# Row maxima that read scores from PSUM, a last maximum over four transposes, and another split of the eight PSUM banks

## The chip, the cores and the metric

The kernel runs on one core of a Trainium2 chip. The core has a matrix engine (TensorE, PE in the rows; its weight loads are PEld), a vector engine (VectorE, DVE), a scalar engine (ScalarE, ACT), a general engine (GpSimd, POOL) and an engine that issues DMAs (SyncE, SP). Matrix products land in PSUM, which this kernel uses as eight banks of 128 partitions by 512 fp32 columns. The metric is device time in microseconds, lower is better.

## The reference, cut to what matters

Three layers follow each other: an attention in which a query sees only keys of the same hash bucket, a gated layer, and a layer with a leaky rectifier.

```python
q_bits = einsum('bhsd,dk->bhsk', q, proj) > 0        # 6 bits; the same for k
mask   = q_bucket[..., :, None] == k_bucket[..., None, :]
scores = where(mask, scale * q @ k.T, -1e9)          # batch 2, 8 heads, 768 x 768, d = 64
attn   = exp(scores - scores.max(-1)) ; attn /= attn.sum(-1) + 1e-9
x      = (attn @ v)          -> 1536 tokens x 512
g      = x @ w_gate          # 512 x 1536
x      = (g * sigmoid(g) * (x @ w_val)) @ w_out      # 1536 x 512
h      = x @ w_in            # 512 x 2048
out    = (max(h, 0) + alpha * min(h, 0)) @ w_out2    # 2048 x 512
```

What the change touches is `scores.max(-1)`: the largest score of each query over its 768 keys.

## The kernel before

**Units.** An attention unit is one head and 256 queries: 48 units, two of them (`x` = 0 and 1) making an item of a head pair. `s_bank` computes scores transposed, keys on partitions and queries along columns: three PSUM banks `S` (j = 0, 1, 2) of 128 x 2 x 256, each of four matmuls (L282, L283), and after each bank ScalarE copies it into the SBUF tile `se` (L284). `s_max` then takes on VectorE the larger of the columns of banks 0 and 1 (L288), with a floor the larger of that and bank 2 (L289), both over 512 columns and both reading `se`, and folds the two halves of 256 columns into one (L291). `s_mt` transposes that result on TensorE, two 128 x 128 transposes (L297, tile `mt`), and a reduction over 256 columns (L299) gives the maximum of each query (`mq`). `s_mb` transposes `mq` back as a broadcast (L304, tile `mb`), `s_sub` subtracts it from `se` (L309, 1536 columns), `s_exp` takes the exponential (L314), and `s_pv` multiplies by the values into `po` (L321, two instructions for each fp32 matmul). The tile `m2`, which holds the maxima, has one buffer; `se` has four.

**Stages.** Tokens go in three chunks of 512. First, attention alone works on chunk 0 (units 0 to 15). Then the gated layer of chunk 0 runs with the attention of chunk 1 between its matmuls, and the gated layer of chunk 1 with the attention of chunk 2 (`RATES` says how many attention steps go with each step of the layer). After that come the gated layer of chunk 2, with no attention left, and the last layer of all three chunks. Below, the stretches are called first (14 to 136 us of the profile), second (136 to 340), third (340 to 495), fourth (495 to 617) and fifth (617 to the end).

**PSUM banks.** A tile takes a bank by its tag, and the next tile of a tag waits until a bank of that tag is free. Before: tag S has two banks, M one, G two, Y two, po one. Scores take S, S, M. In the first stretch `mt` and `mb` take G, the hash products `hp` take po, and `po` takes Y. From the second stretch on, `mt`, `mb` and `hp` all take S, so two banks serve two thirds of the scores and all of these; gates take G (2) and values Y (2), and the products of the gated layer's second weight alternate between them.

**What sets the order.** The kernel is written in Python with the tile framework. The program's text gives each instruction a priority; the framework's scheduler then places the instructions of each engine in a fixed queue, waiting for free buffers and banks, and adds the semaphores. Each engine works through its queue strictly in order. So a change of banks also moves instructions in the queues.

## Time and profile before

| | us |
|---|---|
| median of 3 runs | 887.34 (886.62 to 889.05) |
| the profiled execution, its own time | 884.68 |
| its span, first to last instruction | 882.8 |
| TensorE busy, whole span | 827.7 (94%) |
| VectorE busy | 559.6 (63%) |
| ScalarE busy | 449.3 (51%) |
| GpSimd busy | 373.8 (42%) |

The profiled execution lies 2.66 us below the median of the runs, and 1.9 us of its own time lie outside its span. Busy shares are means over stretches with different limits: TensorE is busy all of the third and fifth stretch, while in the first two VectorE and ScalarE are busy for most of the time as well. A busy TensorE is not TensorE at its peak, since matmuls overlap and their ends are modelled; the distance from the start of one to the start of the next tells what one costs.

### The profile page before, as it was taken

How to read it: one execution, taken by the hardware profiler on the slowest of the kernel's cores; microseconds unless marked ns; L12 is line 12 of the kernel's file. 1: busy time of each engine (PE TensorE's matmuls, PEld its weight loads, DVE VectorE, ACT ScalarE, POOL GpSimd, SP SyncE). 2: the span in 40 equal slices, each digit the busy share in tenths (PEclk: the TensorE clock that was granted, in tenths of full speed). 3: DMA queues.
4: the chain of work that ended last, by engine and by line, in shares of the span. 5: the costliest groups of instructions: out<-in, count | busy, mean ns of one | idle time of the engine just before them, and what ended most of it. 6: DMA issues, size and time to landing. Idle time of an engine off the chain costs nothing.

```text
span 882.8 us, 11030 instructions
## 1 busy us (share of the span) xinstructions
PE 827.7 (94%) x3952; PEld 685.9 (78%) x3952; DVE 559.6 (63%) x824; ACT 449.3 (51%) x738; POOL 373.8 (42%) x304
## 2 busy tenths in 40 slices
PE   5988769988989999999999998999999999999998
PEld 3777658867777788888888787877888888888886
DVE  5788989997789976776767355554633353334332
ACT  6787767577666565555554232413433333334331
POOL 4221443766555443342221354534544454445441
PEclk9999989999999999999999999999999999999999
DMA  9111343775755535745444668878000300010001
GB/s 221 42 45 60 127 160 128 217 236 214 235 199 192 179 131 191 240 148 195 168 179 152 218 253 295 294 282 281 2 1 1 130 14 1 1 48 1 1 1 48
DMA packets 57286, 122.01 MB, mean 138 GB/s; under 512 B 16912, under 2 KB 29200, under 8 KB 56720
## 3 DMA queue, kind: packets, MB, share of 16 engines
q1 hardware_dynamic: 56080, 118.51, 39.3%
q0 software_dynamic: 1008, 2.75, 1.5%
q8 instruction: 31, 0.51, 0.2%
q14 instruction: 23, 0.19, 0.1%
q10 hardware_dynamic: 144, 0.05, 0.0%
HBM read 94.03 MB, written 27.26 MB: 137 GB/s over the span
## 4 chain that ended last, share of the span: by engine, by line
PE 69%; DVE 12%; ACT 7%; DMA 7%; issue 3%; POOL 1%; SPq 0%; DVEq 0%; ACTq 0%; POOLq 0%
PE po L321 9%; PE gp L628 7%; PE gp L629 7%; PE gp L627 7%; PE op L632 5%; PE hp L627 5%; PE hp L628 5%; PE op L633 5%; PE op L634 5%; PE hp L629 5%; PE S L283 2%; DMA raw<-in_wblk_dram 2%; PE S L282 2%; DMA wb<-w 2%; ACT se L314 2%
## 5 line engine op out<-in xcount | busy, mean ns | idle before, releaser
L622 POOL TENSOR_TENSOR gl<-ex,gh 128x512 fp32r<-128x512 f32 x84 | 111.7, 1330 | 182.8 <-ACT gh L619 182.6
L321 PE MATMUL po<-se,vv 128*128 128x256 f32 x576 | 145.9, 389 | 8.6 <-ACT se L314 8.6
L321 PEld LDWEIGHTS po<-se,vv 128*128 128x128 f32 x576 | 107.5, 194 | 26.2 <-ACT se L314 11.4
L627 PE MATMUL gp<-xh,wb 128*128 128x512 f32 x288 | 122.4, 426 | 2.9 <-DMA wb<-w 2.9
L613 DVE TENSOR_SCALAR ex<-hp,al 128x512 f32<-128x512 f32 x48 | 36.0, 751 | 134.8 <-PE hp L629 134.7
L629 PE MATMUL gp<-xh,wb 128*128 128x512 f32 x288 | 114.7, 398 | 0.0
L628 PE MATMUL gp<-xl,wb 128*128 128x512 f32 x288 | 113.9, 396 | 0.1
L619 ACT ACTIVATE gh<-ex 128x512 fp32r<-128x512 f32 x84 | 53.0, 631 | 114.9 <-DVE ex L616 68.4
L529 POOL TENSOR_TENSOR wt<-wt,wr 128x512 int32<-128x512 int32 x48 | 65.5, 1368 | 100.3 <-DVE wt L527 56.5
L564 ACT ACTIVATE wb<-w 128x512 fp32r<-128x512 f32 x96 | 60.4, 631 | 91.8 <-PE hp L629 77.8
L314 ACT ACTIVATE se<-se 128x1536 f32<-128x1536 f32 x48 | 71.3, 1485 | 48.9 <-DVE se L309 48.7
L284 ACT ACTIVATE se<-S 128x512 f32<-128x512 f32 x144 | 80.4, 592 | 25.8 <-PE S L283 22.4
L282 PE MATMUL S<-QA,kt 128*128 128x256 f32 x288 | 82.0, 313 | 9.9 <-ACT se L284 6.2
L309 DVE SCALAR_TENSOR_TENSOR se<-se,mb 128x1536 f32<-128x1536 f32 x48 | 83.7, 1744 | 2.3 <-PE mb L304 2.2
L283 PE MATMUL S<-qb,kt 76*128 76x256 f32 x288 | 75.8, 292 | 3.4 <-ACT qb L204 2.6
L627 PE MATMUL hp<-xh,wb 128*128 128x512 f32 x192 | 74.7, 389 | 0.0
L628 PE MATMUL hp<-xl,wb 128*128 128x512 f32 x192 | 74.7, 389 | 0.0
L629 PE MATMUL hp<-xh,wb 128*128 128x512 f32 x192 | 74.7, 389 | 0.0
L632 PE MATMUL op<-wb,gh 128*128 128x512 f32 x192 | 74.7, 389 | 0.0
L633 PE MATMUL op<-wb,gh 128*128 128x512 f32 x192 | 74.7, 389 | 0.0
L634 PE MATMUL op<-wb,gl 128*128 128x512 f32 x192 | 74.7, 389 | 0.0
L571 POOL TENSOR_TENSOR wb<-w,wb 128x512 fp32r<-128x512 f32 x48 | 61.9, 1289 | 24.1 <-ACT wb L564 24.1
(95 smaller groups left out, 1707.0 us busy)
## 6 DMA issues: line engine op xcount, KB each, us to landing
wb<-w SPq DMA_DIRECT2D x72, 512.0 KB, 4.3
raw<-in_wblk_dram SPq DMA_DIRECT2D x68, 512.0 KB, 4.0
w<-wb SPq DMA_DIRECT2D x36, 512.0 KB, 2.9
qr<-in_q_dram SPq DMA_DIRECT2D x24, 256.0 KB, 2.9
nat<-in_k_dram SPq DMA_DIRECT2D x8, 384.0 KB, 4.5
vv<-in_v_dram SPq DMA_DIRECT2D x16, 192.0 KB, 4.9
whole<-wt SPq DMA_DIRECT2D x12, 256.0 KB, 2.2
w<-whole SPq DMA_DIRECT2D x12, 256.0 KB, 5.7
```

The lines of the kernel that those rows point to most:

```text
L282: nc.tensor.matmul(pt[:, i, :], lhsT=ka[:, sl], rhs=qa, start=True, stop=False)
L283: nc.tensor.matmul(pt[:, i, :], lhsT=kb[:, sl], rhs=qb, start=False, stop=True)
L309: nc.vector.scalar_tensor_tensor(out=u.se, in0=u.se, scalar=FLOOR, in1=u.mx[:, None, :].to_broadcast([P, NC, GQ]), op0=ALU.max, op1=ALU.su ...
L314: nc.scalar.activation(out=u.se, in_=u.se, func=AF.Exp, scale=SCALE)
L321: nc.tensor.matmul(it.po[:, u.x, :], lhsT=VV[it.b, it.p][:, kb, u.x * D:u.x * D + P], rhs=u.se[:, kb, :], start=kb == 0, stop=kb == NC - 1)
L622: nc.gpsimd.tensor_tensor(out=l, in0=ex, in1=f32(h), op=ALU.subtract)
L627: nc.tensor.matmul(pt, lhsT=h, rhs=ah, start=first, stop=False)
L628: nc.tensor.matmul(pt, lhsT=h, rhs=al_, start=False, stop=False)
L629: nc.tensor.matmul(pt, lhsT=l, rhs=ah, start=False, stop=last)
L632: nc.tensor.matmul(pt, lhsT=gh, rhs=h, start=first, stop=False)
L633: nc.tensor.matmul(pt, lhsT=gh, rhs=l, start=False, stop=False)
L634: nc.tensor.matmul(pt, lhsT=gl, rhs=h, start=False, stop=last)
```

## The change

1. L288 and L289 become L291 and L293: one operand of each is now the PSUM bank of scores itself (bank 1 and bank 2) and no longer its copy in `se`. The copies are still made, since L309 needs them. They are written in the text with the scores of the unit, ahead of the top of the unit before.
2. In the first two stretches (`at.halves`) the fold of two halves (L291 before) goes away. Instead all four 128 x 128 pieces are transposed (L303) and the reduction (L304) runs over 512 columns. In the third stretch the fold (L307) and two transposes (L309) stay, with a reduction over 256 columns (L310).
3. Banks: S gets three (scores of all j, and `hp` from the second stretch on), a new tag T one, G two, Y one, po one. In the first stretch `hp` takes T and `po` takes Y and po in turn; from the second on `mt` and `mb` take T. Gates, values and the second weight's products go round three banks G, Y, G in place of four.

```diff
 def s_bank(u, j):
-        pt = at.ps.tile([P, 2, GQ], F32, tag=at.tag["S"][j], name="S", bufs=at.nb[at.tag["S"][j]])
+        pt = at.ps.tile([P, 2, GQ], F32, tag="S", name="S", bufs=at.nb["S"])
+        u.pt.append(pt)
...
-    def s_max(u):
-        nc.vector.tensor_tensor(out=m2, in0=u.se[:, 0:2, :], in1=u.se[:, 2:4, :], op=ALU.max)
-        nc.vector.scalar_tensor_tensor(out=m2, in0=u.se[:, 4:6, :], scalar=FLOOR, in1=m2, op0=ALU.max, op1=ALU.max)
-        u.m1 = m2[:, 0, :]
-        nc.vector.tensor_tensor(out=u.m1, in0=m2[:, 0, :], in1=m2[:, 1, :], op=ALU.max)
+    def s_max(u, j):
+        if j == 1:
+            u.m2 = at.sm.tile([P, 2, GQ], F32, tag="m2", name="m2", bufs=1)
+            nc.vector.tensor_tensor(out=u.m2, in0=u.pt[1], in1=u.se[:, 0:2, :], op=ALU.max)
+        else:
+            nc.vector.scalar_tensor_tensor(out=u.m2, in0=u.pt[2], scalar=FLOOR, in1=u.m2, op0=ALU.max, op1=ALU.max)
...
 def s_mt(u):
+        if at.halves:
+            for j in range(2):
+                for h in range(2):
+                    nc.tensor.transpose(tp[:, j, h, :], u.m2[:, h, j * P:(j + 1) * P], ident)
+            nc.vector.tensor_reduce(out=u.mq, in_=tp.rearrange("p a b c -> p a (b c)"), axis=AX.X, op=ALU.max)
+        else:
+            m1 = u.m2[:, 0, :]
            nc.vector.tensor_tensor(out=m1, in0=m1, in1=u.m2[:, 1, :], op=ALU.max)
            for j in range(2):
                nc.tensor.transpose(tp[:, j, 0, :], m1[:, j * P:(j + 1) * P], ident)
            nc.vector.tensor_reduce(out=u.mq, in_=tp[:, :, 0, :], axis=AX.X, op=ALU.max)
...
 def gate_bank():
+        tag = "GYG"[at.gates % 3]
...
-                tag = ("G", "M", "G", "po")[f % 4]
+                tag = ("G", "Y", "G", "po")[f % 4]
-                    ops = [at.ps.tile([P, 512], F32, tag=t, name="op", bufs=at.nb[t]) for t in "SSYY"]
+                    ops = [at.ps.tile([P, 512], F32, tag=t, name="op", bufs=at.nb[t]) for t in "SSST"]
...
-    at.nb = dict(S=2, M=1, G=2, Y=2, po=1)
-    at.tag = dict(S="SSM", m="G", hp="po", po="Y")
+    at.nb = dict(S=3, T=1, G=2, Y=1, po=1)
+    at.tag = dict(m="G", hp="T", po=("Y", "po"))
-    at.tag = dict(S="SSM", m="S", hp="S", po="po")
+    at.tag = dict(m="T", hp="S", po=("po", "po"))
+        at.halves = c == 0
```

**Where the queues move, VectorE, second stretch.** These are the maxima of one unit before (`m_2421`), with the reduction and the subtraction of units ahead of it. What an instruction waits for stands in brackets, by the engine that releases it.

```order
L299 TENSOR_REDUCE mq<-mt 128x2 [waits PE_49]
L571 TENSOR_TENSOR wb<-wt,wb 128x512 [waits DMAHW0_49,Activation_49]
L198 TENSOR_SCALAR mk<-hp,ck 44x384 [waits PE_49]
L288 TENSOR_TENSOR m_2421<-se 128x512
L525 TENSOR_SCALAR wt<-raw_2413 128x512 [waits DMAHW5_49,DVE_49]
L309 SCALAR_TENSOR_TENSOR se<-se,mb 128x1536 [waits PE_49]
L289 SCALAR_TENSOR_TENSOR m_2421<-se,m_2421 128x512 [waits DVE_49,Activation_49]
L527 SCALAR_TENSOR_TENSOR wt<-raw_2413,wt 128x512 [waits DVE_49]
L291 TENSOR_TENSOR m_2421<-m_2421 128x256 [waits DVE_49]
```

The same place now, for a unit `m_2430`:

```order
L542 SCALAR_TENSOR_TENSOR wt<-raw_2570,wt 128x512 [waits DVE_49]
L291 TENSOR_TENSOR m_2430<-S,se 128x512 [waits PE_49]
L304 TENSOR_REDUCE mq<-mt 128x2
L293 SCALAR_TENSOR_TENSOR m_2430<-S,m_2430 128x512 [waits DVE_49,Activation_49]
L320 SCALAR_TENSOR_TENSOR se<-se,mb 128x1536 [waits PE_49]
L622 SCALAR_TENSOR_TENSOR ex<-ex,gp 128x512 [waits Activation_49]
```

The first maximum of a unit now stands ahead of the reduction of the unit before, whose transposes it waits for, since `m2` has one buffer; the second maximum still waits for ScalarE.

**TensorE, third stretch.** Around the transposes of a unit and the broadcast `mb` of the unit ahead of it, before:

```order
L193 MATMUL hp<-qb_66,sq_65 44x256
L297 MATMUL mt<-ident,m_3527 128x128 [waits DVE_49,Activation_49]
L297 MATMUL mt<-ident,m_3527 128x128
L627 MATMUL gp<-xh,wb 128x512 [waits DMAHW2_49]
L628 MATMUL gp<-xl,wb 128x512
L629 MATMUL gp<-xh,wb 128x512
...
L304 MATMUL mb<-ident,mq 128x128 [waits DVE_49]
```

And now:

```order
L193 MATMUL hp<-qb_66,sq_65 44x256
L309 MATMUL mt<-ident,m_3457 128x128 [waits DVE_49]
L309 MATMUL mt<-ident,m_3457 128x128
L642 MATMUL gp<-xh,wb 128x512 [waits DMAHW2_49]
L643 MATMUL gp<-xl,wb 128x512
L644 MATMUL gp<-xh,wb 128x512
...
L333 MATMUL po<-se,vv 128x256
L315 MATMUL mb<-ident,mq 128x128 [waits DVE_49,PE_49]
```

The places are alike (six gate matmuls between), but `mt` no longer waits for a copy by ScalarE, and `mb`, which now shares the one bank T with `mt`, waits for the reduction that reads `mt`.

**TensorE, first stretch.** Scores and transposes of neighbouring units, before:

```order
L282 MATMUL S<-QA,kt_127 128x256 [waits Activation_49]
L283 MATMUL S<-qb_67,kt_127 128x256
...
L321 MATMUL po<-se,vv 128x256 [waits DMAHW4_49,Activation_49]
L297 MATMUL mt<-ident,m_620 128x128 [waits DVE_49,PE_49]
L297 MATMUL mt<-ident,m_620 128x128
L304 MATMUL mb<-ident,mq 128x128 [waits PE_49]
```

And now:

```order
L283 MATMUL S<-QA,kt_124 128x256 [waits DVE_49]
L284 MATMUL S<-qb_66,kt_124 128x256
...
L333 MATMUL po<-se,vv 128x256 [waits DMAHW5_49,Activation_49]
...
L283 MATMUL S<-QA,kt_124 128x256 [waits DVE_49,PE_49]
...
L303 MATMUL mt<-ident,m_684 128x128 [waits PE_49]
L303 MATMUL mt<-ident,m_684 128x128 x3
L315 MATMUL mb<-ident,mq 128x128 [waits DVE_49]
```

The scores of the next unit now wait for VectorE, whose maxima hold banks 1 and 2 of the unit before, and no longer for ScalarE's copies alone.

## Rows read from the trace of the kernel before

**Rows 1.** Page: the span, and ScalarE's copies (busy us, mean ns | idle before).
```profile
span 882.8 us, 11030 instructions
...
L284 ACT ACTIVATE se<-S 128x512 f32<-128x512 f32 x144 | 80.4, 592 | 25.8 <-PE S L283 22.4
```

**Rows 2.** Stretches: busy us (instructions) of PE, PEld, DVE, ACT, POOL; PEclk, DMA, GB/s.
```profile
14.00:136.00 122.00, 100.04 (x538) 80.95 (x538) 103.87 (x157) 92.83 (x155) 35.09 (x28) 0.97 0.32 94
136.00:340.00 204.00, 188.72 (x954) 157.87 (x952) 175.59 (x255) 139.18 (x233) 110.51 (x86) 0.97 0.58 192
340.00:495.00 155.00, 154.97 (x794) 132.55 (x793) 106.83 (x163) 79.42 (x129) 44.83 (x36) 1.00 0.52 183
```

**Rows 3.** VectorE groups, 0 to 340 us: busy us, mean ns | idle before, releaser.
```profile
L288 DVE TENSOR_TENSOR m<-se 128x512 f32<-128x512 f32 x35 | 33.0, 944 | 4.0 <-ACT se L284 4.0
L289 DVE SCALAR_TENSOR_TENSOR m<-se,m 128x512 f32<-128x512 f32 x35 | 29.7, 848 | 1.4
L291 DVE TENSOR_TENSOR m<-m 128x256 f32<-128x256 f32 x35 | 16.8, 480 | 0.5
L299 DVE TENSOR_REDUCE mq<-mt 128x2 f32<-128x256 f32 x34 | 14.2, 417 | 9.7 <-PE mt L297 9.5
L607 DVE SCALAR_TENSOR_TENSOR ex<-ex,gp 128x512 f32<-128x512 f32 x12 | 8.2, 679 | 2.2 <-ACT ex L604 2.1
```

**Rows 4.** One line each over the whole span: ns min/median/max, first and last start.
```profile
L288 DVE TENSOR_TENSOR m<-se x48: 639/686/2666, 16.7 to 470.4; 128x512 f32<-128x512 f32 x48
L289 DVE SCALAR_TENSOR_TENSOR m<-se,m x48: 649/692/2266, 20.0 to 471.9; 128x512 f32<-128x512 f32 x48
L607 DVE SCALAR_TENSOR_TENSOR ex<-ex,gp x36: 650/682/690, 148.8 to 603.8; 128x512 f32<-128x512 f32 x36
```

**Rows 5.** The chain that ended last, shares by line: 0 to 340, then 340 to 495.
```profile
by line: PE po L321 12.3%; issue 7.7%; PE gp L628 5.2%; PE gp L629 5.0%; PE gp L627 4.9%; ACT se L314 4.7%; DVE se L309 4.4%; DMA kt<-in_k_dram 4.2%; PE S L283 3.8%; PE S L282 3.7%; ACT se L284 3.5%; DVE wt L527 2.8%; DVE m L288 2.6%; DVE m
by line: PE po L321 26.7%; PE gp L629 18.8%; PE gp L627 18.8%; PE gp L628 18.8%; PE S L283 5.6%; PE S L282 5.5%; PE mb L304 2.1%; PE mt L297 2.0%; PE hp L192 0.9%; PE hp L193 0.8%; issue 0.0%
```

**Rows 6.** Timeline at 72 us: start, us, engine, line, what, idle before and its releaser.
```profile
72.40 0.38 PE L297 MATMUL mt<-ident,m 128*128 128x128 f32 x2
72.62 0.38 PE L304 MATMUL mb<-ident,mq 128*128 128x128 f32 x2
72.82 0.42 DVE L299 TENSOR_REDUCE mq<-mt 128x2 f32<-128x256 f32 x1 [0.36 <-PE mt L297]
```

**Rows 7.** TensorE's waits, 0 to 340 us: us in total, times, longest.
```profile
PE S L282 <- ACT se L284: 6.2, 7, 3.3
...
PE mt L297 <- ACT se L284: 3.2, 2, 2.8
...
PE S L282 <- DVE se L309: 1.7, 2, 1.5
```

**Rows 8.** Timelines of PE and DVE: second maxima (units 16, 38), scores (17, 39).
```profile
117.60 0.28 PE L283 MATMUL S<-qb,kt 76*128 76x256 f32 x1
...
127.73 2.27 DVE L289 SCALAR_TENSOR_TENSOR m<-se,m 128x512 f32<-128x512 f32 x1
...
376.38 1.58 DVE L289 SCALAR_TENSOR_TENSOR m<-se,m 128x512 f32<-128x512 f32 x1
...
384.19 0.28 PE L282 MATMUL S<-QA,kt 128*128 128x256 f32 x1
```

**Rows 9.** Timeline of a gate bank: last matmul, its last reader, third group after it.
```profile
567.35 0.39 PE L629 MATMUL gp<-xh,wb 128*128 128x512 f32 x1
...
570.51 0.68 DVE L607 SCALAR_TENSOR_TENSOR ex<-ex,gp 128x512 f32<-128x512 f32 x1
...
573.02 0.39 PE L627 MATMUL gp<-xh,wb 128*128 128x512 f32 x1
```

**Rows 10.** Two of the stretches with a lower granted clock, columns as in rows 2.
```profile
120.00:140.00 20.00, 15.86 (x73) 12.73 (x73) 16.82 (x23) 10.01 (x16) 7.99 (x6) 0.85 0.40 123
...
180.00:200.00 20.00, 18.15 (x85) 14.85 (x85) 19.14 (x27) 14.61 (x27) 14.90 (x12) 0.91 0.71 223
```

More of the change, by code (lines that the diff above doesn't have):

```diff
@@ L284, in s_bank @@
         nc.scalar.activation(out=u.se[:, 2 * j:2 * j + 2, :], in_=pt, func=AF.Copy)
[L286 to L291 removed]
+    def s_max(u, j):
[4 more added lines that the diff above has]
+            nc.vector.scalar_tensor_tensor(out=u.m2, in0=u.pt[2], scalar=FLOOR, in1=u.m2, op0=ALU.max, op1=ALU.max)
+            u.pt = None
     def s_mt(u):
[L295 to L297 removed]
+        tp = at.ps.tile([P, 2, 2, P], F32, tag=at.tag["m"], name="mt", bufs=at.nb[at.tag["m"]])
         u.mq = at.sm.tile([P, 2, 1], F32, tag="mq", name="mq", bufs=2)
[L299 removed]
+        if at.halves:
[5 more added lines that the diff above has]
+            m1 = u.m2[:, 0, :]
+            nc.vector.tensor_tensor(out=m1, in0=m1, in1=u.m2[:, 1, :], op=ALU.max)
+            for j in range(2):
+                nc.tensor.transpose(tp[:, j, 0, :], m1[:, j * P:(j + 1) * P], ident)
+            nc.vector.tensor_reduce(out=u.mq, in_=tp[:, :, 0, :], axis=AX.X, op=ALU.max)
     def s_mb(u):
@@ L318, in s_pv @@
         if j == 0 and u.x == 0:
-            it.po = at.ps.tile([P, 2, GQ], F32, tag=at.tag["po"], name="po", bufs=at.nb[at.tag["po"]])
+            tag = at.tag["po"][it.i % 2]
+            it.po = at.ps.tile([P, 2, GQ], F32, tag=tag, name="po", bufs=at.nb[tag])
         for kb in (2 * j, 2 * j + 1):
@@ L363, in lsh_attention_moe_kernel @@
     at.alone = True
+    at.halves = True
     def attention():
@@ L408, in top @@
         def top(u):
-            s_max(u)
             s_mt(u)
@@ L644, in out_rows, with gate_bank @@
         nc.sync.dma_start(out=out[r0:r0 + P, :], in_=ob)
-    def gate_bank(tag):
+    def gate_bank():
+        tag = "GYG"[at.gates % 3]
+        at.gates += 1
         return at.ps.tile([P, W], F32, tag=tag, name="gp", bufs=at.nb[tag])
@@ L680, in stage1 @@
             for tag in "GY":
-                pt = gate_bank(tag)
+                pt = gate_bank()
                 w = w_next()
@@ L758, in lsh_attention_moe_kernel @@
     VV = {}
-    at.nb = dict(S=2, M=1, G=2, Y=2, po=1)
-    at.tag = dict(S="SSM", m="G", hp="po", po="Y")
+    at.nb = dict(S=3, T=1, G=2, Y=1, po=1)
+    at.tag = dict(m="G", hp="T", po=("Y", "po"))
+    at.gates = 0
     pr = wp.tile([P, 2, 44], F32, tag="wr", name="pr", bufs=2)
```

12 lines of the change are left out of this document (5 added, 7 removed).

## The prediction

> **What bounds the kernel now.** I read first the busy time of the engines by stretch [rows 2], then the chain that ended last in the stretches of interest [rows 5], then the groups on VectorE and TensorE's waits [rows 3, 7]. The span is 882.8 us [rows 1]. Only the first three stretches hold attention, so only they hold the edited instructions; in the fourth and fifth the change renames banks and nothing else. The third stretch is TensorE's alone: it is busy for 154.97 of 155 us and the chain there names no other engine [rows 2, 5]. VectorE is busy for 106.8 of those 155 us, so time taken from it there buys nothing, and a stall put on TensorE there costs its full length. The first two stretches are of another kind. TensorE is busy for 100.0 of 122 and 188.7 of 204 us, VectorE for 103.9 and 175.6, 85% and 86%. Neither is full; the chain passes from one to the other and through ScalarE [rows 5]. A gain has to come from here.
>
> **The maxima from PSUM.** Before, the four VectorE instructions of a unit take 0.944 + 0.848 + 0.480 + 0.417 = 2.69 us on average up to 340 us [rows 3]. The two long ones are uneven: the medians are 0.686 and 0.692 us, the worst 2.67 and 2.27 [rows 4]. Instructions of the same 512 columns that read one operand from PSUM are even: L607 goes from 0.650 to 0.690 us and averages 0.679 [rows 3, 4]. So I put L291 and L293 at 0.68 us each. The reduction over 512 columns is not in the trace; it costs no less than the one over 256 (0.417 us) and, by the nearest instruction with 512 PSUM columns, about 0.68; I take 0.68, the row of its own width. A unit then costs 3 x 0.68 = 2.04 us, which saves 0.65 us; 32 units in the first two stretches make 20.8 us of VectorE time. The third stretch saves on its two maxima only, and there it is hidden behind TensorE.
>
> [...]
>
> How much of 20.8 us arrives has wide bounds. Nothing arrives if VectorE merely waits longer; at most its busy share does, 86% or 17.9 us. L288 gives the nearest measure: 2.6% of 340 us, 8.8 us, of its 33.0 us lie on the chain, 27% [rows 3, 5]. I take that share of 20.8 us: **5.6 us gained**. What the maxima wait for does not change: the program order still has them wait for ScalarE, whose copies of the same banks come first, so I count no earlier start.
>
> **Two more transposes.** Two transposes start 0.22 us ahead of the next pair [rows 6], so one costs 0.11 us of TensorE, and 64 more cost 7.0 us. All of them fall in the first two stretches. TensorE's share of the chain there, summed over the lines that the row shows before it breaks off, is 34.9%, and some is cut off [rows 5]; I charge 40%: **2.8 us lost**. Bounds are 0 and 7.0 us. They lie between the second maximum and the reduction, which already left VectorE idle for 9.5 us [rows 3].
>
> **Banks.** From the second stretch on `mt` and `mb` leave tag S. Waits that came from that sharing are `mt` on ScalarE's copies, 3.2 us, and scores on the subtraction that reads `mb`, 1.7 us [rows 7]: 4.9 us, of which I take **4 us gained**, since something else may be late next (the scores' wait on copies, 6.2 us, stays) [rows 7]. Bounds: 0 and 4.9.
>
> The single bank T adds a wait: `mb` now waits for the reduction of the following unit, and in VectorE's queue that stands behind another unit's first maximum. After the last transpose comes its end (0.27 us, the 0.38 of a pair less half of 0.22), then 0.68 and 0.68 us on VectorE, 1.63 in all [rows 3, 6]. TensorE has six gate matmuls and a transpose to fill this. Twelve matmuls of a gate start to start take some 2.7 us: the bank of [rows 9] has its last matmul at 567.35; two groups of twelve follow, and the third group after it starts at 573.02, 5.67 us for 25 steps, 0.227 each. So it has 6 x 0.227 + 0.11 = 1.47 us, and 0.16 us is missing. Over 16 units of the second stretch that is 2.6 us; in the third, where the reduction stays at 0.42 us, 1.37 against 1.47 leaves nothing. I take **2 us lost**. What is queued behind the waiting `mb` is all of TensorE's queue, gates included. The upper bound adds one long VectorE instruction's half, 0.85 us (L288's worst is above 2 us), to each of 32 units: 27 us.
>
> Gates and values lose one bank of four. Of the 108 groups I compared the last read with the start of the third group after it. The tightest place is in [rows 9]: the bank is read until 571.19 and would be needed at 573.02, 1.83 us later. So three banks suffice everywhere, at no cost; the cover is the next two groups' 5.4 us of matmuls. Outside attention the renamed banks keep their numbers.
>
> **The sum.** -5.6 + 2.8 - 4 + 2 = -4.8 us. [...] I count a third, 1.6 us, for idle time that goes away. In all -6.4 us: the profiled execution's own 884.68 us would become 878.3. It stands 2.66 us below the median of 887.34, and against the median I forecast 887.34 - 6.4 = 880.9, say 881.
>
> **The rivals.** *VectorE's time arrives in full.* VectorE is busy for 86% of the first two stretches, and if it is their limit, 17.9 us arrive and not 5.6: 881 - 12.3 = 869. For it speaks that 20 us at a time are above 95% (19.14 in the slice from 180) [rows 10]; against it, that the chain holds only 27% of L288.
>
> *It is hidden.* The shorter maxima turn into longer waits for the transposes, as the 9.5 us of waiting at the reduction suggest [rows 3]. Then -4 + 2.8 + 2 = +0.8, 888, within 0.3% (2.7 us) of before, about what a measurement of this kernel can tell from no change.
>
> *Scores lose their head start, and it is slower.* Before, a bank of scores is free as soon as ScalarE copied it, and TensorE runs ahead: the last scores of unit 17 start at 117.60 us, while the second maximum of unit 16 ends only at 130.00 [rows 8]. Now bank 1 and bank 2 are held until VectorE read them, and TensorE's queue stands still at the next scores, with `po`, `mt` and `mb` behind. The price is a round trip for each unit: four score matmuls (0.11 us each, by the transposes' 0.22 for two) and ScalarE's copy of 0.592 us [rows 1, 6], 1.03 us, if VectorE has nothing else to do meanwhile. 32 units make 33 us at worst. At a third of that, 11 us, the result is 892. It decides from (6.4 + 2.7) / 32 = 0.28 us a unit. Against it: once the gates run, the scores come late enough anyway, as at unit 39, whose third bank starts at 384.19 us, 6.2 us after the second maximum of unit 38 ended [rows 8], and VectorE has other work queued.
>
> *The change doesn't do what it says:* the maxima keep their 0.9 us since something else than the second SBUF operand made them uneven. Then the 5.6 us shrink to the fold's 0.48 less 0.26 for the wider reduction, 0.22 x 32 x 27% = 1.9 us, and the time is 885, which falls in with the hidden case or just beyond.
>
> **How the numbers follow.** The forecast (881, own range 875 to 884.6) has 0.45, VectorE in full (866 to 875) 0.15, hidden or not as told (884.7 to 890) 0.18, slower (890 to 900) 0.22, the lost head start being most of that and the bank T the rest. So faster by over 0.3% has 0.60, no change 0.18, slower 0.22. For 8 in 10 the range goes from 870, leaving out some 0.06 of the second case, to 891, leaving out some 0.14 of the slower one.
>
> **What would show it.** In the changed profile: L291, L293 and L304 at 0.65 to 0.69 us without outliers (right), or with any above 1 us (wrong). VectorE's busy time in the first two stretches down by about 20 us. The scores' matmuls waiting for VectorE's maxima in the first stretch: under 5 us in total if the forecast holds, over 10 if the head start mattered. `mb` waiting for the reduction L304 in the second stretch: 2 to 3 us, and none in the third for L310; more than 5 us there would sink the forecast. The second stretch should end some 6 us earlier, with the later ones as long as before; a third stretch in which TensorE is idle for more than 2 us would make the prediction wrong.

## The result, and the profile after

The changed kernel takes 873.82 us (median of 4 runs, 872.72 to 877.4) beside 886.98 us for the kernel before on the same chip: ratio 0.9854, 95% interval 0.9824 to 0.9884, 13.2 us less. Two later sets on other chips gave 0.9898 (0.9867 to 0.9929) and 0.9885 (0.9864 to 0.9906). So the gain lies between some 10 and 13 us. The forecast was 881, a gain of 6.4 us: the direction was right, the size half of what came.

Where it went is seen if both profiles are cut at the same events: the starts of the subtractions of units 0, 15, 31 and 47 (L309 before, L320 after). The first three rows are the kernel before, the next three the changed one. Columns are start:end, length, then busy us (instructions) of PE, PEld, DVE, ACT and POOL, granted clock, DMA share, GB/s; they answer to [rows 2].

```profile
23.80:132.40 108.60, 89.07 (x491) 71.91 (x490) 93.49 (x144) 82.12 (x137) 31.32 (x26) 0.97 0.25 83
132.40:322.50 190.10, 174.82 (x881) 145.96 (x880) 167.36 (x243) 130.89 (x220) 105.58 (x83) 0.97 0.58 192
322.50:482.60 160.10, 160.07 (x832) 137.38 (x831) 112.35 (x170) 85.70 (x138) 48.52 (x39) 1.00 0.52 183
```

```profile
24.30:122.40 98.10, 85.39 (x512) 72.56 (x511) 77.55 (x120) 77.85 (x131) 24.51 (x21) 0.98 0.23 76
122.40:309.90 187.50, 175.89 (x928) 147.20 (x927) 158.94 (x236) 133.61 (x226) 105.97 (x87) 1.00 0.64 209
309.90:470.20 160.30, 159.47 (x827) 134.88 (x827) 103.23 (x165) 85.52 (x138) 45.70 (x38) 1.00 0.50 176
```

**The first stretch** became 10.5 us shorter, the second 2.6, the third stayed (TensorE idles 0.8 us in it), and the 400 us behind it stayed too. The changed program was profiled four more times in the experiments (twice as it is, twice with edits in the fifth stretch alone); with this one its first stretch took 98.1, 96.6, 96.6, 96.8 and 96.7 us (mean 97.0, so 11.6 less than before) and its second 187.5, 188.3, 191.6, 190.1 and 191.1 (mean 189.7, 0.4 less). So the gain is mainly one of the first stretch, where attention runs alone. The kernel before has a single profile, of a run 2.3 us below its median (884.68 and 886.98), so some 2 us more may have been gained in the second. In the rows of the first stretch TensorE's idle time fell from 19.5 us (108.60 less 89.07) to 12.7, its busy time from 89.1 to 85.4. VectorE's busy time in both stretches fell by 24.4 us, where about 20 were forecast. From here on "first" and "second" mean these two, 15 and 16 units.

VectorE's edited instructions in the changed kernel: groups of 0 to 340 us as in [rows 3], then one line each over the whole span, ns min/median/max, as in [rows 4].

```profile
L293 DVE SCALAR_TENSOR_TENSOR m<-S,m 128x512 f32<-128x512 f32 x36 | 24.4, 678 | 1.0 <-ACT se L285 0.6
L291 DVE TENSOR_TENSOR m<-S,se 128x512 f32<-128x512 f32 x36 | 24.4, 676 | 12.3 <-ACT se L285 6.9 <-PE mt L303 5.2
L304 DVE TENSOR_REDUCE mq<-mt 128x2 f32<-128x512 f32 x35 | 23.7, 678 | 7.7 <-PE mt L303 7.6
```

```profile
L291 DVE TENSOR_TENSOR m<-S,se x48: 632/682/693, 16.9 to 457.6; 128x512 f32<-128x512 f32 x48
L293 DVE SCALAR_TENSOR_TENSOR m<-S,m x48: 642/681/693, 19.9 to 458.5; 128x512 f32<-128x512 f32 x48
L304 DVE TENSOR_REDUCE mq<-mt x35: 650/681/692, 21.9 to 328.3; 128x2 f32<-128x512 f32 x35
```

The durations are those forecast, 0.68 us, and the long ones are gone. TensorE's waits in the changed kernel, 0 to 340 us (total, times, longest), as in [rows 7]:

```profile
PE mb L315 <- DVE mq L304: 9.8, 10, 2.1
...
PE po L333 <- ACT se L325: 3.7, 4, 2.2
...
PE S L283 <- ACT se L285: 1.6, 3, 0.7
...
PE S L283 <- DVE m L291: 0.9, 2, 0.8
```

Scores hardly wait for the maxima (0.9 us), and their wait for ScalarE's copies fell from 6.2 to 1.6. In their place `mb` waits 9.8 us for the reduction of the next unit, through the single bank T, all of it in the second stretch: 2 to 3 us were forecast. One such place in the changed kernel, TensorE's row and VectorE's rows (start, us, ...):

```profile
157.51 0.60 PE L303 MATMUL mt<-ident,m 128*128 128x128 f32 x4
...
162.13 0.40 PE L315 MATMUL mb<-ident,mq 128*128 128x128 f32 x2 [2.07 <-DVE mq L304]
```

```profile
159.27 0.69 DVE L622 SCALAR_TENSOR_TENSOR ex<-ex,gp 128x512 f32<-128x512 f32 x1
160.19 0.60 DVE L540 TENSOR_SCALAR wt<-raw 128x512 int32<-128x512 int32 x1 [0.23 <-DMA raw<-in_wblk_dram]
160.71 0.68 DVE L291 TENSOR_TENSOR m<-S,se 128x512 f32<-128x512 f32 x1
161.31 0.67 DVE L304 TENSOR_REDUCE mq<-mt 128x2 f32<-128x512 f32 x1
```

The transposes have ended by 158.1 us. VectorE reaches the reduction at 161.31, behind an instruction of the gates (L622), a weight conversion (L540), which itself waited 0.23 us for a DMA, and another unit's first maximum. The prediction counted the maximum and left the other two out.

### The profile page after: what moved, and what is told of

Its sections match the earlier page's. It is cut to its first block, busy times and chain, and to the rows that moved or that the text cites. A ratio compares the mean times of both kernels' runs of the same rounds, so it can differ in the third digit from the quotient of the medians.

```text
span 871.5 us, 11218 instructions
## 1 busy us (share of the span) xinstructions
PE 824.7 (95%) x4022; PEld 685.0 (79%) x4022; DVE 525.4 (60%) x789; ACT 448.4 (51%) x738; POOL 364.5 (42%) x304
## 4 chain that ended last, share of the span: by engine, by line
PE 62%; DVE 12%; DMA 10%; ACT 9%; issue 4%; POOL 2%; SPq 0%; ACTq 0%; DVEq 0%; POOLq 0%
PE po L333 8%; DMA raw<-in_wblk_dram 7%; PE gp L643 6%; PE gp L642 6%; PE gp L644 6%; PE op L648 5%; PE hp L643 5%; PE hp L644 5%; PE op L647 5%; PE op L649 5%; PE hp L642 5%; DMA wb<-w 2%; PE S L283 2%; PE S L284 2%; ACT se L285 2%
## 5 line engine op out<-in xcount | busy, mean ns | idle before, releaser
L333 PE MATMUL po<-se,vv 128*128 128x256 f32 x576 | 143.6, 384 | 3.7 <-ACT se L325 3.7
L642 PE MATMUL gp<-xh,wb 128*128 128x512 f32 x288 | 121.2, 421 | 4.0 <-DMA wb<-w 3.9
L644 PE MATMUL gp<-xh,wb 128*128 128x512 f32 x288 | 113.1, 393 | 0.0
L643 PE MATMUL gp<-xl,wb 128*128 128x512 f32 x288 | 112.9, 392 | 0.0
L544 POOL TENSOR_TENSOR wt<-wt,wr 128x512 int32<-128x512 int32 x48 | 63.5, 1327 | 87.3 <-DVE wt L542 44.7
L285 ACT ACTIVATE se<-S 128x512 f32<-128x512 f32 x144 | 80.2, 592 | 22.9 <-PE S L284 19.1
L320 DVE SCALAR_TENSOR_TENSOR se<-se,mb 128x1536 f32<-128x1536 f32 x48 | 83.8, 1746 | 3.2 <-PE mb L315 3.1
```

The lines of the kernel that those rows point to most:

```text
L285: nc.scalar.activation(out=u.se[:, 2 * j:2 * j + 2, :], in_=pt, func=AF.Copy)
L320: nc.vector.scalar_tensor_tensor(out=u.se, in0=u.se, scalar=FLOOR, in1=u.mx[:, None, :].to_broadcast([P, NC, GQ]), op0=ALU.max, op1=ALU.su ...
L333: nc.tensor.matmul(it.po[:, u.x, :], lhsT=VV[it.b, it.p][:, kb, u.x * D:u.x * D + P], rhs=u.se[:, kb, :], start=kb == 0, stop=kb == NC - 1)
L642: nc.tensor.matmul(pt, lhsT=h, rhs=ah, start=first, stop=False)
L643: nc.tensor.matmul(pt, lhsT=h, rhs=al_, start=False, stop=False)
L644: nc.tensor.matmul(pt, lhsT=l, rhs=ah, start=False, stop=last)
```

## The experiments

The theory going in was that one term had been mis-sized: the share of VectorE's time that arrives (27%), the banks, or the clock. (Read in steps of 0.2 us, the granted clock of the kernel before is 1.00 from 14 to 345 us but for five pieces of 3.4 us at 0.50, from 119.3, 129.5, 191.0, 218.3 and 255.8 us. Each begins within 1.6 us of the end of a TensorE wait of 1.3 to 3.3 us.) The table gathers what the texts below refer to. Ratios are against the kernel before on the same chip; lengths of the first and second stretch, in us, come from one profile each. The changed kernel itself repeats within 1.5 us in the first and 4.1 in the second, so smaller differences say nothing.

| kernel | ratio [95%] | first | second |
|---|---|---|---|
| before | 1 | 108.6 | 190.1 |
| changed, mean of five | 0.985 to 0.990 | 97.0 | 189.7 |
| e1, banks alone | 1.0036 [1.0013, 1.0059] | 108.0 | 190.8 |
| e2, PSUM operand and order alone | 0.9898 [0.9875, 0.9921] | 102.1 | 187.1 |
| e3, four transposes alone | 0.9929 [0.9908, 0.9949] | 102.7 | 190.3 |
| e8, changed, old banks | 0.9924 [0.9900, 0.9948] | 99.2 | 191.4 |
| e4, changed, fold kept | 0.9971 [0.9947, 0.9995] | 101.7 | 194.4 |
| e5, changed, maxima from SBUF | 1.0188 [1.0145, 1.0230] | 97.2 | 211.1 |
| e7, changed, maxima at their old place | 0.9923 [0.9896, 0.9950] | 102.8 | 186.7 |
| e9, two T banks, two gate banks | 0.9924 [0.9894, 0.9954] | 99.7 | 191.7 |
| e10, two T banks, two S banks | 0.9974 [0.9952, 0.9996] | 104.7 | 191.8 |
| e13, a third maximum on the chain | 1.0146 [1.0122, 1.0170] | 109.3 | 202.5 |
| e14, the same beside the chain | 0.9925 [0.9903, 0.9948] | 103.5 | 191.1 |
| e15, transposes made twice | 1.0055 [1.0036, 1.0074] | 102.0 | 200.9 |
| e17, before, reduction made twice | 1.0067 [1.0043, 1.0090] | 112.9 | 190.9 |
| e18, before, transposes made twice | 1.0097 [1.0074, 1.0120] | 111.1 | 191.2 |

### One part alone

**e1**, the banks of the change in the kernel before.

```diff
-    at.nb = dict(S=2, M=1, G=2, Y=2, po=1)
-    at.tag = dict(S="SSM", m="G", hp="po", po="Y")
+    at.nb = dict(S=3, T=1, G=2, Y=1, po=1)
+    at.tag = dict(m="G", hp="T", po=("Y", "po"))
...
-    at.tag = dict(S="SSM", m="S", hp="S", po="po")
+    at.tag = dict(m="T", hp="S", po=("po", "po"))
```

> The kernel before with the change's bank split alone (3 for S, 3 for gates and values, 1 for po, 1 for T). Prediction's terms: the sharing waits go (-4), the wait of mb for the reduction comes (+2, or less since the fold stays and the reduction is the narrow one): 883 to 885 against 887.0, ratio 0.996 to 0.998. Rival 1 (the banks are the mis-sized term: the waits of mt, scores and po on ScalarE's copies end TensorE's long gaps, and with them the half-clock pieces): -7 us or more, ratio under 0.992, granted clock 0.995 or above. Rival 2 (VectorE's time is the mis-sized term): as the prediction's terms, ratio 0.996 to 1.0.

Measured: 3 us slower. TensorE's waits in it, 0 to 330 us:

```profile
PE mb L304 <- DVE mq L299: 10.7, 7, 2.3
PE po L322 <- ACT se L314: 8.4, 10, 2.6
...
PE S L282 <- ACT se L284: 6.2, 7, 3.0
```

The new wait is here in full, while `po` and scores wait as before (6.2 us for the copies). So in the kernel before the banks' net of -2 us had the wrong sign.

**e2**, maxima from PSUM at their new place in the text; fold, two transposes and banks as before.

```diff
-        nc.vector.tensor_tensor(out=m2, in0=u.se[:, 0:2, :], in1=u.se[:, 2:4, :], op=ALU.max)
+            nc.vector.tensor_tensor(out=u.m2, in0=u.pt[1], in1=u.se[:, 0:2, :], op=ALU.max)
...
                 s_bank(u, j)
+                if j == 2:
+                    s_max(u, 1)
```

> The kernel before with the two maxima from PSUM alone, in the change's order; the fold, the two transposes and the old banks stay. VectorE saves (0.944 + 0.848 - 2 x 0.678) us x 32 units = 14 us in the first two stretches. Prediction's share of 27%: -3.8 us, ratio 0.996. Rival 1 (banks): the same or nothing. Rival 2 (VectorE's time arrives by its busy share of 86%): -12 us, ratio 0.987. If scores lose their head start in the old banks (S has two there), slower than before.

Measured: 9 us faster, between the two theories; 6.5 us of the profile's gain lie in the first stretch.

**e3**, four transposes and the wide reduction in the first two stretches; the rest as before.

```diff
-        nc.vector.tensor_tensor(out=u.m1, in0=m2[:, 0, :], in1=m2[:, 1, :], op=ALU.max)
...
+                for h in range(2):
+                    nc.tensor.transpose(tp[:, j, h, :], u.m2[:, h, j * P:(j + 1) * P], ident)
```

> The kernel before with four transposes and the wide reduction in the first two stretches alone; maxima still read se, banks as before. VectorE saves (0.480 + 0.417 - 0.678) x 32 = 7 us, TensorE gains 64 transposes, 7 us. Prediction's shares: -1.9 + 2.8 = +0.9 us, ratio 1.001. Rival 2 (VectorE's time arrives by 86%): -6 + 2.8 = -3.2 us, ratio 0.996. A third possibility, that TensorE's added work is no loss in stretches where it idles: -2 to -6 us.

Measured: 6 us faster, all of it in the first stretch. The forecast had this part as a small loss.

### One part left out

**e8**, the changed kernel with the banks of before (e1's diff the other way round).

> The changed kernel with the banks of before (S has two, mt and mb in G, then S). What is lost against the changed kernel (873.8) is the banks' worth in its presence. Prediction's terms: 2 us (876). Rival 1 (banks are the mis-sized term): 7 us or more, 881 or above, and the half-clock pieces come back. Rival 2 (VectorE's time): under 2 us, 873 to 876.

Measured: 0.9924, some 2 to 6 us worse than the changed kernel. Together with e1: the same bank split costs 3 us in the kernel before and is worth some 4 in the changed one. The parts do not add.

**e4**, the changed kernel with the fold and two transposes everywhere (`at.halves = False`).

> The changed kernel with the fold and two transposes kept throughout: banks and maxima from PSUM together. If the parts added, e1 (+3 us) and e2 (-9 us) would give -6, 880, ratio 0.993. If VectorE's time is what counts, whatever the banks: about e2's 876. If the banks are worth something only once VectorE is shorter (as the changed kernel's 873.8 against 879.3 with the old banks suggests): under 876, ratio 0.988 or less.

Measured: 0.9971, 7 to 10 us worse than the changed kernel, in both stretches.

**e5**, the changed kernel with the maxima reading `se`.

```diff
-            nc.vector.tensor_tensor(out=u.m2, in0=u.pt[1], in1=u.se[:, 0:2, :], op=ALU.max)
+            nc.vector.tensor_tensor(out=u.m2, in0=u.se[:, 2:4, :], in1=u.se[:, 0:2, :], op=ALU.max)
...
-            nc.vector.scalar_tensor_tensor(out=u.m2, in0=u.pt[2], scalar=FLOOR, in1=u.m2, op0=ALU.max, op1=ALU.max)
+            nc.vector.scalar_tensor_tensor(out=u.m2, in0=u.se[:, 4:6, :], scalar=FLOOR, in1=u.m2, op0=ALU.max, op1=ALU.max)
```

> The changed kernel with both maxima reading se in SBUF, at the same places in the order: banks, order and four transposes together. If the parts added, e1 (+3) and e3 (-6) give -3, 882, ratio 0.997. If the operand in PSUM is what makes the maxima even, L291 and L293 are uneven again, with means of 0.85 to 0.95 us and single ones above 2 us; then the result is 9 us or more above the changed kernel (873.8). If instead the earlier issue of the maxima is what counts, it stays within 3 us of it.

Measured: 15 us slower than before, 25 slower than the changed kernel. First the maxima (0 to 345 us), then the whole span's L291, then TensorE's largest wait, then the two stretches:

```profile
L291 DVE TENSOR_TENSOR m<-se 128x512 f32<-128x512 f32 x35 | 36.2, 1036 | 10.9 <-ACT se L285 7.6 <-PE mt L303 3.1
...
L293 DVE SCALAR_TENSOR_TENSOR m<-se,m 128x512 f32<-128x512 f32 x35 | 31.4, 898 | 0.7
```

```profile
L291 DVE TENSOR_TENSOR m<-se x48: 637/692/2972, 16.8 to 484.4; 128x512 f32<-128x512 f32 x48
```

```profile
PE mb L315 <- DVE mq L304: 25.2, 13, 5.9
```

```profile
25.00:122.20 97.20, 85.78 (x512) 73.66 (x511) 81.64 (x120) 77.27 (x130) 25.74 (x22) 0.96 0.23 74
122.20:333.30 211.10, 184.44 (x926) 153.11 (x925) 176.97 (x236) 134.63 (x227) 112.62 (x86) 0.95 0.56 187
```

The second SBUF operand is what makes the maxima uneven: same place in the order, other operand, 1036 and 898 ns in place of 676 and 678. What they meet is GpSimd. One long maximum of e5, the GpSimd instructions beside it, and the `mb` behind it (start, us, ...):

```profile
219.96 1.71 POOL L184 TENSOR_TENSOR qb<-qr,QA 64x512 fp32r<-64x512 f32 x1
220.47 2.97 DVE L291 TENSOR_TENSOR m<-se 128x512 f32<-128x512 f32 x1
221.64 1.25 POOL L544 TENSOR_TENSOR wt<-wt,wr 128x512 int32<-128x512 int32 x1
...
224.19 0.66 PE L315 MATMUL mb<-ident,mq 128*128 128x128 f32 x2 [5.93 <-DVE mq L304]
```

The maximum ends at 223.44, 0.55 us behind the second GpSimd instruction (222.89). Of e5's 96 maxima 39 took more than 0.75 us, and each of them overlaps a GpSimd instruction in the trace; of the other 57 only 13 do. In the changed kernel 64 of 96 overlap one, and none is long.

The stretches part. In the first, where GpSimd is busy for 25.7 us of 97, the operand is worth nothing (97.2 against 97.0). In the second, where it is busy for 112.6 of 211, it is worth 21 us, at a granted clock of 0.95 in place of 0.98 to 1.00, and `mb` waits 25.2 us in place of 9.8. In the first, `mt` and `mb` also have the two banks of G. Which of these differences decides wasn't tested.

**e7**, run like e4 and e5 beside the changed kernel (e0), has both maxima written where they stood before, just ahead of the transposes.

```diff
         def banks(u):
-                if j == 2:
-                    s_max(u, 1)
-            s_max(u, 2)
...
         def top(u):
+            s_max(u, 1)
+            s_max(u, 2)
             s_mt(u)
```

> The changed kernel with both maxima issued where they stood before (just ahead of the transposes) and still reading PSUM: separates the operand from the place in VectorE's order. If the operand's evenness is the whole gain of the maxima, 873 to 875. If the earlier place counts, slower: VectorE stands at the second maximum's wait for the last scores less often now, and the scores' banks are held longer, 3 us or more above, with scores waiting for maxima over 5 us in the first two stretches.

> The changed kernel again, beside the three kernels above on one chip: 873 to 874 us, ratio 0.985. Its runs give more pairs of granted clock and time: where the time follows the clock inside one kernel, about 4 us for 0.008 of clock, as its four runs show so far (873.3 at 0.997, 877.4 at 0.988).

Measured: 878.79 beside 876.31 us of the changed kernel on the same chip, two ratios with overlapping intervals. By the profiles the first stretch loses 5.8 us by the old place; the second is 3.0 shorter, less than the 4.1 within which it repeats. The groups of VectorE (0 to 330 us), first here, then in the changed kernel's run beside it:

```profile
L291 DVE TENSOR_TENSOR m<-S,se 128x512 f32<-128x512 f32 x35 | 23.7, 677 | 4.5 <-ACT se L285 4.4
...
L304 DVE TENSOR_REDUCE mq<-mt 128x2 f32<-128x512 f32 x34 | 23.2, 683 | 13.1 <-PE mt L303 12.9
```

```profile
L291 DVE TENSOR_TENSOR m<-S,se 128x512 f32<-128x512 f32 x36 | 24.3, 676 | 14.5 <-ACT se L285 8.6 <-PE mt L303 5.6
...
L304 DVE TENSOR_REDUCE mq<-mt 128x2 f32<-128x512 f32 x35 | 23.7, 678 | 4.6 <-PE mt L303 4.5
```

At the old place VectorE waits 13.1 us before the reduction, for transposes that it has only just made possible (9.7 us in the kernel before [rows 3]); at the new place 4.6 us. But its first maximum waits 14.5 us there in place of 4.5, so VectorE's idle time before the two has moved (17.6 and 19.1 us) and not shrunk. TensorE's waits in e7's first stretch (23.3 to 126.1 us) show more:

```profile
PE po L333 <- ACT se L325: 4.5, 6, 1.9
PE S L283 <- DVE m L291: 3.5, 8, 0.8
```

In the changed kernel's run beside it the first of these is 2.1 us and the second under 0.3: the later a maximum is issued, the longer it holds the scores' bank. TensorE's idle time as a whole grew by only 2.8 us, so not all of the 5.8 is traced. The prediction had said that what the maxima wait for doesn't change, and had counted no earlier start.

### A second bank for T

**e9** takes it from gates and values, **e10** from the scores.

```diff
-    at.nb = dict(S=3, T=1, G=2, Y=1, po=1)
-    at.tag = dict(m="G", hp="T", po=("Y", "po"))
+    at.nb = dict(S=3, T=2, G=1, Y=1, po=1)
+    at.tag = dict(m="T", hp="G", po=("Y", "po"))
...
-        tag = "GYG"[at.gates % 3]
+        tag = "GY"[at.gates % 2]
```

```diff
-                    ops = [at.ps.tile([P, 512], F32, tag=t, name="op", bufs=at.nb[t]) for t in "SSST"]
+                    ops = [at.ps.tile([P, 512], F32, tag=t, name="op", bufs=at.nb[t]) for t in "SSTT"]
...
-    at.nb = dict(S=3, T=1, G=2, Y=1, po=1)
+    at.nb = dict(S=2, T=2, G=2, Y=1, po=1)
```

> The changed kernel with a second bank for mt and mb (T has two), taken from the gates and values (two in place of three). If the single bank T is what holds back the rest, the 9 us of mb waiting for the reduction go, and with them 3 to 6 us: 868 to 872, ratio 0.980 to 0.985. If two gate banks are too few, gates wait for VectorE's reads (at the tightest place by 1.83 - 2.7 = -0.9 us a time), and it is no faster or slower: 876 or above. If VectorE is simply full, mb's wait turns into a wait elsewhere: 874 to 877.

> The changed kernel with the second bank for mt and mb taken from the scores (S two, T two). The wait of mb goes as in the run beside it. If scores need the third bank (a unit's three banks held until ScalarE and VectorE read them), scores wait for VectorE's maxima by several us in all and it is 876 or above; if not, 868 to 872.

Measured: neither better than the changed kernel, which ran on other chips: e9 is behind it by 0.3 to 0.7%, with intervals that partly overlap, e10 by 0.8 to 1.2%. The wait of `mb` for the reduction is gone from the leading waits of both, and others have come. TensorE's waits from 0 to 330 us, e9 and then e10:

```profile
PE S L284 <- ACT qb L204: 5.8, 3, 2.3
PE S L283 <- ACT se L285: 3.9, 4, 2.2
PE po L333 <- ACT se L325: 3.5, 4, 2.0
```

```profile
PE hp L192 <- DVE m L291: 7.8, 5, 2.8
...
PE S L283 <- ACT se L285: 6.3, 11, 1.3
```

In e10 the hash products, which share S with the scores, now wait for the first maximum to release a bank. So the 9.8 us of `mb` were not 9.8 us to be had: with the eight banks there are, taking that wait away makes another, and neither version beats the changed kernel.

### What lowers the granted clock

**e11** makes TensorE pause 24 times in the fifth stretch, where it works alone: a transpose, 13 copies on VectorE, and a transpose of what they give, for which TensorE waits. **e12** puts 27 transposes and the same copies in the same places, with nothing waiting. In both, the first products of the last layer leave bank Y to the pauses. This is e11's edit, cut:

```diff
+    def pause():
+        z = at.ps.tile([P, P], F32, tag="Y", name="zz", bufs=at.nb["Y"])
+        for _ in range(1):
+            nc.tensor.transpose(z, ident, ident)
+        nc.vector.tensor_copy(out=fin.z, in_=z)
+        for _ in range(12):
+            nc.vector.tensor_copy(out=fin.z, in_=fin.z)
+        z = at.ps.tile([P, P], F32, tag="Y", name="zz", bufs=at.nb["Y"])
+        nc.tensor.transpose(z, fin.z, ident)
...
-                tag = ("G", "Y", "G", "po")[f % 4]
+                tag = ("G", "po")[f % 2]
...
+                if f % 2 == 0:
+                    pause()
```

> The changed kernel, in whose last stretch (TensorE alone, granted clock 1.00) 24 pauses are put: TensorE waits for a chain of 13 copies on VectorE, some 2.5 us each. Theory 'gaps lower the clock': pieces of half granted clock appear behind a good part of the pauses, up to 3.4 us each, and a pause costs more than its own length, by up to 1.7 us: granted clock of the stretch 0.85 to 0.95, and the kernel 60 us for the pauses and 10 to 40 us more. Rival (the half-clock pieces have nothing to do with idle time of TensorE): granted clock stays at 0.99 or above, and the time grows by the pauses alone.

> The same places and the same chain of copies on VectorE, but TensorE is kept busy with 27 transposes (0.11 us each, 2.9 us) in place of waiting. Theory: no pieces of half clock, granted clock 0.99 or above, and each place costs its 2.9 us and no more, 70 us in all. Rival: as many pieces as with the pauses.

Measured: 935.44 and 947.81 us beside the changed kernel's 876.31 on another chip. The fifth stretch, e11 first, then e12 (columns as above):

```profile
606.00:930.00 324.00, 281.02 (x1204) 222.41 (x1202) 206.18 (x465) 91.96 (x146) 119.97 (x93) 0.98 0.04 15
```

```profile
608.00:944.00 336.00, 333.31 (x1802) 285.84 (x1800) 184.93 (x464) 90.64 (x146) 118.04 (x93) 1.00 0.04 17
```

The clock stayed at 1.00 where TensorE was kept busy and fell where it paused: less than forecast (0.98, not 0.85 to 0.95). TensorE waited 42.9 us in all, 1.8 a pause, and a low piece followed only some of the pauses (0.02 of 324 us is 6.5 us, by an estimate four pieces like the one below). One of them in e11, TensorE's timeline (start, us, ...):

```profile
615.58 0.33 PE L726 MATMUL zz<-ident,zs 128*128 128x128 f32 x1 [2.79 <-DVE zs L724]
...
616.60 0.39 PE L643 MATMUL hp<-xl,wb 128*128 128x512 f32 x1
616.83 0.42 PE L644 MATMUL hp<-xh,wb 128*128 128x512 f32 x1
617.07 0.61 PE L642 MATMUL hp<-xh,wb 128*128 128x512 f32 x1
617.47 0.63 PE L643 MATMUL hp<-xl,wb 128*128 128x512 f32 x1
617.90 0.63 PE L644 MATMUL hp<-xh,wb 128*128 128x512 f32 x1
...
620.46 0.41 PE L644 MATMUL hp<-xh,wb 128*128 128x512 f32 x1
620.71 0.39 PE L642 MATMUL hp<-xh,wb 128*128 128x512 f32 x1
```

After 2.79 us of waiting the matmuls come 0.23 us apart, then 0.43, about half the pace, then 0.23 again. Eight matmuls from 617.07 to 620.46 took 3.39 us in place of 8 x 0.23 = 1.84: such a piece costs 1.55 us where TensorE sets the pace.

### The price of one instruction on a unit's chain

**e13** adds a third maximum, which repeats the second's operand, to the 36 units whose maxima are written while `at.halves` holds; **e14** adds the same instruction but lets nobody use its result; **e15** makes each of the four transposes twice, in the 35 units that have them. **e16** is the changed kernel again beside them.

```diff
+            if at.halves:
+                nc.vector.tensor_tensor(out=u.m2, in0=u.pt[2], in1=u.m2, op=ALU.max)
```

```diff
+            if at.halves:
+                nc.vector.tensor_tensor(out=u.pt[2], in0=u.pt[2], in1=u.m2, op=ALU.max)
```

```diff
-                for h in range(2):
+                for h in (0, 1, 0, 1):
```

> The changed kernel with a third maximum of 512 columns from PSUM in each of the 36 units that have four transposes (it repeats the last operand, so the maximum stays what it was): 36 x 0.68 = 24.5 us more of VectorE, on the chain between the second maximum and the transposes. By the prediction's share of 27%: +6.6 us, 882. If VectorE's time arrives by its busy share there (83%): +20 us, 895. If VectorE waits for others anyway: under +3 us.

> The same added instruction, but its result goes back into the scores' bank, which nobody reads any more: as much VectorE time, but nobody waits for the result (the bank comes free later in both). If VectorE's sum of work is the limit, as much as in the run above. If the latency of a unit's chain counts, less than half of it.

> The changed kernel with each of the four transposes made twice (the second into the same place): 36 x 4 x 0.11 = 16 us more of TensorE in the first two stretches. By the prediction's 40%: +6.3 us, 882. If added work of TensorE is free where it idles, 875 to 878; it could even be a gain if it keeps the granted clock up.

> The changed kernel again, beside the three above: 873 to 877, ratio 0.985 to 0.990.

Measured: 901.04, 880.43 and 892.51 us beside 876.88. The first two stretches of e13, then of e14:

```profile
24.80:134.10 109.30, 91.09 (x512) 75.35 (x510) 90.80 (x137) 76.05 (x128) 23.34 (x21) 0.94 0.18 63
134.10:336.60 202.50, 182.12 (x929) 150.52 (x929) 172.06 (x253) 135.38 (x228) 108.32 (x87) 0.97 0.60 196
```

```profile
24.10:127.60 103.50, 89.12 (x512) 73.94 (x510) 90.39 (x134) 76.39 (x129) 23.45 (x21) 0.96 0.20 68
127.60:318.70 191.10, 178.03 (x930) 148.78 (x929) 174.64 (x254) 135.72 (x228) 110.89 (x87) 0.99 0.64 209
```

VectorE is as busy in e14 as in e13 (90.39 and 90.80; 174.64 and 172.06), and yet e14 is 20.6 us faster. Where the unit's next step waits for the instruction, it costs 24.2 us for 36 x 0.68 = 24.5 us of work, 99%; beside the chain 3.5 us, 14%. The transposes, on the chain as well, cost 15.6 us for 140 x 0.11 = 15.4.

The two stretches differ in this. Beside e16's profile, on the same chip (96.6 and 191.6 us), e13 is longer by 12.7 and 10.9 us, e14 by 6.9 in the first and nothing in the second (0.5 less), for some 11 us of added work in each. So in the second stretch it is the waiting alone that costs. In the first, VectorE's time costs more than half its length even if nobody waits for the result. The granted clock went down with it (0.94 in e13's first stretch, 0.96 in e14's, 0.98 in the changed kernel's), and both hold a scores' bank longer; what these add to either price isn't separated.

**e17** and **e18** ask the same of the kernel before: its reduction made twice, or its two transposes made twice, in the 35 units up to the third stretch (by the trace 35 more reductions and 70 more transposes).

```diff
-        nc.vector.tensor_reduce(out=u.mq, in_=tp, axis=AX.X, op=ALU.max)
+        for _ in range(2 if at.halves else 1):
+            nc.vector.tensor_reduce(out=u.mq, in_=tp, axis=AX.X, op=ALU.max)
```

```diff
-        for j in range(2):
+        for j in (0, 1, 0, 1) if at.halves else (0, 1):
             nc.tensor.transpose(tp[:, j, :], u.m1[:, j * P:(j + 1) * P], ident)
```

> The kernel before with the reduction of the transposed maxima made twice in the 34 units of the first two stretches: 34 x 0.417 = 14.2 us more of VectorE, on each unit's chain. Theory 'the chain of a unit sets the pace': +12 to +16 us, 898 to 902. The prediction's share of 27%: +3.8 us, 890 or 891.

> The kernel before with its two transposes of a unit made twice in the 34 units of the first two stretches: 68 x 0.11 = 7.5 us more of TensorE, on each unit's chain, as the change adds. Theory 'the chain of a unit sets the pace': +6 to +9 us, 893 to 896. The prediction's 40%: +3 us, 890. If TensorE's added work is free there, as the four transposes without the fold (-6 us) might suggest: 0.

Measured: 890.65 and 893.35 beside 885.42 us. The reduction costs 5.2 us for 35 x 0.417 = 14.6 (36%), between the two forecasts: on a unit's chain, but far from in full. By stretch it is 4.3 us in the first and 0.8 in the second. In the second TensorE's gates stand between the reduction and `mb`, and in the kernel before `mb` hardly waits, so there was room, it seems. The transposes cost 7.9 us for 7.7, but the two stretches show only 3.6 us of it; the profiled execution lost 2.0 us before unit 0's subtraction and more behind the second stretch. So e18 doesn't settle the price in the kernel before.

## Why the prediction missed, point by point

The step that failed is what the first two parts were given: 5.6 us gained as 27% of VectorE's 20.8 us, with no earlier start, less 2.8 us for the transposes, in all a gain of 2.8 us. Made alone, the two parts brought 9.0 and 6.3 us (e2, e3); the whole change brought 10 to 13 where 6.4 were forecast.

**The durations** were right: 0.68 us forecast, 676 to 678 ns, none above 0.693. (The units were 35, not 32: the trace has 35 reductions L304.) e5 shows the other side: a first maximum with both operands in SBUF took up to 2.97 us, beside GpSimd, against 0.69 with one from PSUM. An operand from PSUM adds nothing that the medians show: 682 ns from PSUM and 692 from SBUF (L291 in the changed kernel and in e5).

**The share of VectorE's time** is the term that was mis-sized. The prediction took 27% of it, the part of L288 that lies on the chain that ended last, for both stretches alike. That chain says who came last in one execution; it is not the price of an instruction. The prices measured run from 14% beside a unit's chain to 99% on it in the changed kernel (e14, e13); in the kernel before, one instruction on the chain cost 36% (e17). Part one alone brought 9.0 us where the same term gave 3.8 (e2), part two 6.3 where the same terms gave a loss of 0.9 (e3). With e17's 36% the 5.6 us would have been 7.5, so the share alone does not make up the miss. How much of e2's 9.0 us is time on the chain and how much the earlier place wasn't separated in the kernel before.

**One share for two stretches** hid where it would come. By the prediction's own terms the first stretch should have gained 2.2 us (half of 5.6, less half of 2.8, half of the clock's 1.6, and no banks) and the second 4.2. The first gained 11.6 and the second about nothing. Both looked alike in [rows 2], with VectorE at 85 and 86%. They differ in what stands beside the chain: in the second TensorE has gates to work on. e14 shows the difference too: 6.9 us in the first stretch and nothing in the second for the same instruction.

**No earlier start** was a step that failed on its own: the place in the text is worth 5.8 us of the first stretch by the profiles (e7). Of the whole time it is 2.5 us, not clear of noise.

**The transposes** at 40% were too cheap for the changed kernel, where more of them cost their full time (e15). That they nevertheless came with a gain of 6 us (e3) is only half explained. VectorE's busy time in the first stretch fell by 8.3 us there, from 93.49 to 85.24, while the swap of the fold for a wider reduction takes away 16 x 0.22 = 3.5. The rest lies in instructions that weren't edited: 16 second maxima took 10.9 us in place of 14.0 and 12 weight conversions 6.9 in place of 10.2, while the first maxima went from 11.8 to 13.4. Why the new order of the queue made these shorter stays open.

**Bank T**: the wait came at its named place and for the named reason, but with 9.8 us, not 2.6, because other work of VectorE stands before the reduction too. (In the third stretch it was 0.8 us, where none was forecast.) The prediction said that over 5 us would sink the forecast. The kernel got faster all the same, since other waits went at the same time (the scores' for copies 6.2 to 1.6, `po`'s for the exponential 8.6 to 3.7, `mt`'s 3.2 to none) and e9 and e10 show that this wait is not additive. The banks' net of -2 us was +3 in the kernel before (e1) and about -4 in the changed one (e8): a bank split has no price of its own.

**Three gate banks** suffice, as worked out: TensorE's rows in the changed kernel show no more than one wait of 0.3 us for an instruction that reads a gate bank (L622). **The third stretch** stayed, as forecast.

**The clock** may be under-sized as well; by how much is open. No run shows its 1.6 us: it is the author's estimate, a third of the 20 x (0.15 + 0.09) = 4.8 us that the clocks of 0.85 and 0.91 in [rows 10] make. What the profiles and runs show in its place is this. Five profiles of the same program have second stretches of 187.5 us at a granted clock of 1.00, 188.3 and 190.1 at 0.99, 191.1 and 191.6 at 0.98: with two hundredths of 190 us, 3.8, go 3.6 to 4.1 us, and between the extremes TensorE's busy time makes 3.2 of the 4.1 (175.89 and 179.06). Before, both stretches were at 0.97, which by the same measure is 298.7 x 0.03 = 9.0 us; after, at a mean of 0.98 and 0.99, it is 97.0 x 0.02 + 189.7 x 0.01 = 3.8. Some 5 us in place of 1.6 would come from there. The runs say less. In the three sets of the changed kernel (15 runs) the time falls by 0.15 to 0.4 us for each thousandth of the whole run's granted clock, and not by the 0.87 of full arrival; from 0.981, the median of 79 runs before, to 0.990 after, that is 1.3 to 3.7 us. So the forecast's 1.6 isn't refuted. e11 and e12 show the cause, idle TensorE: a clock of 0.98 where it waited 42.9 us in all, 1.00 where it was kept busy. It is a share of the gain of each part, not one beside them.

**Scores' head start**, the rival on the slow side, didn't come: 0.9 us of waiting. The rival in which VectorE's time arrives in full came closest to the size (869). e14 speaks for a part of it in the first stretch (6.9 us for some 11 of work that nobody waits for) and against it in the second (nothing).

Settled are the durations, the second SBUF operand as what makes the maxima uneven, that the place in the order counts in the first stretch, and that in the changed kernel an instruction on a unit's chain costs far more than the same one beside it. That the chain is also why the two parts together brought more than forecast is argued from this; in the kernel before, e17 shows a third and e18 nothing clear. Not settled is an exact split: the scheduler lays out the queues anew for every version, parts alone add to -9.0 - 6.3 + 3.2 = -12 us, near the 10 to 13 measured, while pairs of parts (e4: -2.5, e8: -7) do not.

## What to carry to other kernels

Price an edit by whether the next step of the same unit waits for it, stretch by stretch, and not by its share of one profile's chain of waits: the same VectorE instruction cost 24 us on the chain and 3.5 beside it, by the profiles all of it in the stretch where attention runs alone. Where a queue is strictly in order, look at what else stands ahead of the instruction that releases a bank, all of it, DMA waits included. And an operand's home that makes an instruction uneven has no one price: here it cost nothing in one stretch and 21 us in the next.
